# Channel attention with a GELU feed-forward layer: the first layer's weights moved by 64 bytes within a partition

## The chip, the cores and the metric

The kernel runs on one core of a Trainium2 chip. The metric is the device time of one execution in microseconds (us). The time of a version is the median of its runs; a profile shows one further execution of the same program.

## The reference, cut to what matters

```python
def _attn_ref(q, k, v, tau):                 # B, N, C = 4, 6080, 256
    qn = q / (np.linalg.norm(q, axis=1, keepdims=True) + 1e-06)
    kn = k / (np.linalg.norm(k, axis=1, keepdims=True) + 1e-06)
    s = kn.transpose(0, 2, 1) @ qn / tau     # 256 x 256 per batch
    s = s - s.max(-1, keepdims=True)
    a = np.exp(s)
    a /= a.sum(-1, keepdims=True) + 1e-09
    return (v @ a).astype(np.float32)

def _moe_ref(x, w_in, w_out):                # x: 24320 x 256, w_in: 256 x 2048, w_out: 2048 x 256
    h = x @ w_in
    g = 0.5 * h * (1.0 + erf(h * np.float32(1.0 / np.sqrt(2.0))))
    return (g @ w_out).astype(np.float32)
```

The result is `_moe_ref(_attn_ref(q, k, v, tau).reshape(24320, 256), w_in, w_out)`.

## The kernel before, in words

For each of the four batches the kernel works out the 256 x 256 attention matrix and multiplies it with `w_in`. The product is that batch's first-layer weight, 256 x 2048, so that `v` goes straight into the first layer. Every operand of the large products is split into a high and a low float32r part, and a product is three matmuls: high by high, low by high, high by low.

**First layer.** The 2048 columns of the weight are cut into four groups of 512 (`NWG`), the 6080 tokens of a batch into six pairs of blocks (`PAIRS`: five with 512 tokens a block, one with 480). A unit is one pair with 256 columns of the weight; there are 4 x 6 x 8 = 192 units. In a unit the 2 x 2 blocks of the weight meet the 2 x 2 blocks of `v`. The eight units of the very first pair do eight block products (`plain_products`); the other 184 do seven (`first_products`), with sums and differences of blocks formed ahead. That makes 8 x 8 + 184 x 7 = 1352 products. Each is three matmuls in `product`, lines 450 to 452: the weight block is the stationary operand that TensorE loads, `v`'s block (`vh`, `vl`) is the moving operand that streams through with 512 or 480 columns. The weights lie in the tiles `wh0` to `wh3` and `wl0` to `wl3`, seven blocks of 1024 bytes a partition in each. Of the plain products 16 take their weight block from another place: block A21 has no slot there and is put into the tiles that later hold `vh4` and `vl4`, or `vh5` and `vl5`. In the trace these are the rows of lines 450 to 452 whose inputs read `vh,vh`, `vl,vh` and `vh,vl`.

**Second layer.** `second_products`, lines 533 to 535, multiplies the GELU of each block (`gh`, `gl`, moving) with a unit's part of `w_out` (`wo`, stationary). A unit has 24 of these matmuls. `product` yields after each three, so that on TensorE's queue a unit's first-layer threes alternate with the second-layer threes of the unit before: 450, 451, 452, 533, 534, 535.

**Around it.** For the next batch, `burst` (lines 191 and 193) adds up scores between the units, with both operands from `hl`, and `w_group` (lines 377 to 379) makes the next weights, with `eh` and `el` stationary and `win` moving. For the first batch these stages stand ahead, with plain float32 matmuls of 256 columns in two passes each (lines 149 and 161). `sum_up` (line 172) is eight matmuls of one column against a column of ones; `softmax` uses their result. The order of all this is the order in which the program is written; TensorE's queue takes it as it stands.

**Where tiles begin.** A pool's tiles lie one behind the other in a partition, each rounded up to 32 bytes, and pools lie in the order in which they are opened. In the built program `wh0` begins at byte 1152, `wl0` at 8320, `wh1` to `wh3` and `wl1` to `wl3` at 185984, 200320, 214656, 193152, 207488 and 221824: multiples of 128, all of them. The three buffers of `wo` begin at 32896, 36992 and 41088, multiples of 128 too, and so does `win`. The moving operands `vh`, `vl`, `gh` and `gl` begin 64 bytes past a multiple of 128, and so do `hl`, `eh`, `el` and the float32 `raw` tiles. (To a multiple of 256, `vh` and `vl` lie 192 past, `gh` and `gl` 64, `wh`, `wl` and `wo` 128.) Every block within a tile starts a multiple of 512 bytes further on, so it lies as its tile does. In the pool `pwh` a tile named `pad` of 64 bytes (line 634) stands ahead of `wh1`.

Of the kernel before, what the change touches and what calls it, by code (L numbers as in the profile page):

```python
# [9 lines left out]
F32 = mybir.dt.float32  # L10
# [6 lines left out]
P = 128  # L17
# [43 lines left out]
def channel_attention_gelu_ffn(ctx, tc, qk, kqt, vt, tau, w_in, w_out, out):  # L61
# [11 lines left out]
    nc = tc.nc  # L73
    const = ctx.enter_context(tc.tile_pool(name="const", bufs=1))
# [3 lines left out]
    ptau = ctx.enter_context(tc.tile_pool(name="ptau", bufs=1))  # L78
# [3 lines left out]
    ps_h = ctx.enter_context(tc.tile_pool(name="ps_h", bufs=4, space=bass.MemoryType.PSUM))  # L82
    ps_o = ctx.enter_context(tc.tile_pool(name="ps_o", bufs=4, space=bass.MemoryType.PSUM))

    whs = [const.tile([P, 7, 2, P], F32R, name="wh0")]
    wls = [const.tile([P, 7, 2, P], F32R, name="wl0")]
    taut = ptau.tile([P, 1], F32, name="taut")
    rtau = ptau.tile([P, 1], F32, name="rtau")
    pstart = tc.tile_pool(name="pstart", bufs=1)
    pst = pstart.__enter__()  # L90

# [4 lines left out]
    make_identity(nc, ident)  # L96
    ones = const.tile([P, P], F32, name="ones")
    nc.gpsimd.memset(ones, 1.0)

    state = {}  # L100

# [68 lines left out]
    def sum_up(nps, acc, start, stop):  # L170
        for i in range(2 * NCT):
            nc.tensor.matmul(nps[:, i:i + 1], acc[:, i // NCT, i % NCT * P:(i % NCT + 1) * P],
                             ones[:, 0:1], start=(start and i == 0), stop=stop, skip_group_check=True)


    hls = {}
# [101 lines left out]
    def softmax(first, pool, name):  # L278
# [14 lines left out]
        if first:  # L293
            nps, acc = ps_o.tile([P, NT], F32, name="po"), state.pop("acc")
            with behind("scores"):
                for j in range(JS):
                    sum_up(nps, acc[:, j], j == 0, j == JS - 1)
            nc.vector.reduce_sum(out=z, in_=nsum[:, :, NSQ // NSJ:NSC], axis=AX.X)
            nc.vector.tensor_tensor(out=x, in0=nps[:, 0:2 * NCT], in1=z, op=ALU.add)
        else:  # L300
            nc.vector.reduce_sum(out=x, in_=nsum[:, :, 0:NSC], axis=AX.X)
# [329 lines left out]
    state["filled"] = True  # L631
    pg = ctx.enter_context(tc.tile_pool(name="pg", bufs=5))
    pwh = ctx.enter_context(tc.tile_pool(name="pwh", bufs=1))
    pwh.tile([P, 16], F32, name="pad")
    for g in range(1, NWG):
        whs.append(pwh.tile([P, 7, 2, P], F32R, name=f"wh{g}"))
        wls.append(pwh.tile([P, 7, 2, P], F32R, name=f"wl{g}"))
# [110 lines left out]
```

## Time and profile before

| | |
|---|---|
| median of three runs | 2212.24 us (2207.69 to 2212.78) |
| the profiled execution's own time | 2208.33 us |
| its span, first to last instruction | 2206.5 us |
| TensorE busy with matmuls | 2182.0 us, 99% of the span |
| VectorE, ScalarE, GpSimd busy | 1387.1, 1432.3 and 1.3 us |
| granted TensorE clock, mean | 0.999 |

A matmul's shown length is modelled and longer than its share of the queue, since matmuls overlap. What a matmul costs is read from the distance between one start and the next, here called a step. The timeline gives starts to 0.01 us.

### The profile page before, as it was taken

The numbers are of one execution on the slowest core, as the hardware profiler recorded it, in microseconds if no ns is written. First come the engines' busy times: TensorE is split into PE (matmuls) and PEld (weight loads), VectorE is DVE, ScalarE is ACT, GpSimd is POOL, SyncE is SP. The second block draws the span as 40 slices with busy tenths as digits, with TensorE's granted clock in tenths as the row PEclk, the third lists the DMA queues.
The fourth block names the chain that finished last, engine by engine and source line by source line (L and its number), as shares of the span: only waits on it lengthen the run. The fifth ranks groups of instructions, "written<-read, shape, count | busy, mean of one in ns | idle before, by whom it ended". The sixth has DMA issues, their size and how long they took to land.

```text
span 2206.5 us, 26233 instructions
## 1 busy us (share of the span) xinstructions
PE 2182.0 (99%) x9664; PEld 1792.7 (81%) x9664; DVE 1387.1 (63%) x2175; ACT 1432.3 (65%) x2599; POOL 1.3 (0%) x8
## 2 busy tenths in 40 slices
PE   8999999999999999999999999999999999999999
PEld 6787778888888888888888888888888888888888
DVE  6985757666576665765667657567466555554554
ACT  5668886557876565665766656656576666666665
POOL 0000000000000000000000000000000000000000
PEclk9999999999999999999999999999999999999999
DMA  9567774232652332322234323232132122122221
GB/s 381 201 218 239 242 251 136 78 113 95 231 197 77 124 105 86 115 94 87 86 105 142 101 82 123 67 124 95 48 105 95 57 91 72 68 87 70 72 76 48
DMA packets 77632, 269.61 MB, mean 122 GB/s; under 512 B 7744, under 2 KB 9792, under 8 KB 75456
## 3 DMA queue, kind: packets, MB, share of 16 engines
q1 hardware_dynamic: 77504, 267.94, 35.9%
q8 instruction: 76, 1.25, 0.2%
q14 instruction: 52, 0.43, 0.1%
HBM read 234.62 MB, written 33.29 MB: 121 GB/s over the span
## 4 chain that ended last, share of the span: by engine, by line
PE 87%; ACT 6%; DMA 5%; DVE 2%; issue 0%; SPq 0%; ACTq 0%; DVEq 0%
PE po L535 15%; PE po L533 14%; PE po L534 14%; PE ph L452 13%; PE ph L451 13%; PE ph L450 12%; DMA kqc<-kqt 4%; PE ph L191 2%; ACT kqc L209 2%; ACT gh L458 1%; ACT g L459 1%; PE ph L193 1%; DMA raw<-qk 1%; DVE acc L139 1%; PE ph L377 1%; PE ph L379 1%
## 5 line engine op out<-in xcount | busy, mean ns | idle before, releaser
L460 DVE TENSOR_TENSOR gl<-g,gh 128x512 fp32r<-128x512 f32 (+1 forms) x768 | 522.8, 682 | 157.7 <-ACT g L459 155.5
L535 PE MATMUL po<-gh,wo 128*128 128x512 f32 (+1 forms) x1536 | 605.2, 394 | 0.0
L533 PE MATMUL po<-gh,wo 128*128 128x512 f32 (+1 forms) x1536 | 599.3, 390 | 4.4 <-ACT gh L458 4.3
L534 PE MATMUL po<-gl,wo 128*128 128x512 f32 (+1 forms) x1536 | 595.9, 388 | 0.5 <-DVE gl L460 0.5
L488 DVE TENSOR_TENSOR h<-ph,p 128x512 f32<-128x512 f32 (+1 forms) x368 | 251.6, 684 | 526.0 <-PE ph L452 415.2
L458 ACT ACTIVATE gh<-h 128x512 fp32r<-128x512 f32 (+1 forms) x552 | 345.7, 626 | 285.0 <-DVE h L488 281.8
L450 PE MATMUL ph<-vh,wh 128*128 128x512 f32 (+1 forms) x1336 | 522.1, 391 | 7.6 <-ACT p L483 3.2
L452 PE MATMUL ph<-vh,wl 128*128 128x512 f32 (+1 forms) x1336 | 522.8, 391 | 0.0
L451 PE MATMUL ph<-vl,wh 128*128 128x512 f32 (+1 forms) x1336 | 521.6, 390 | 0.0
L483 ACT COPY p<-ph 128x512 f32<-128x512 f32 (+1 forms) x368 | 213.2, 583 | 247.7 <-PE ph L452 247.5
L533 PEld LDWEIGHTS po<-gh,wo 128*128 128x128 f32 x1536 | 288.6, 188 | 66.5 <-ACT gh L458 5.4
L534 PEld LDWEIGHTS po<-gl,wo 128*128 128x128 f32 x1536 | 288.5, 188 | 64.9 <-DVE gl L460 0.9
L535 PEld LDWEIGHTS po<-gh,wo 128*128 128x128 f32 x1536 | 288.4, 188 | 61.2
L459 ACT ACTIVATE g<-h 128x512 f32<-128x512 f32 (+1 forms) x552 | 337.6, 612 | 0.0
L450 PEld LDWEIGHTS ph<-vh,wh 128*128 128x128 f32 x1336 | 251.1, 188 | 66.5 <-ACT p L483 6.4
L451 PEld LDWEIGHTS ph<-vl,wh 128*128 128x128 f32 x1336 | 251.2, 188 | 55.9
L452 PEld LDWEIGHTS ph<-vh,wl 128*128 128x128 f32 x1336 | 251.1, 188 | 50.9
L483 ACT COPY u<-ph 128x512 f32<-128x512 f32 (+1 forms) x184 | 106.9, 581 | 114.5 <-PE ph L452 114.5
L458 ACT ACTIVATE gh<-ph 128x512 fp32r<-128x512 f32 (+1 forms) x216 | 124.9, 578 | 22.9 <-PE ph L452 22.7
L488 DVE TENSOR_TENSOR h<-ph,u 128x512 f32<-128x512 f32 (+1 forms) x184 | 125.6, 683 | 3.4
L459 ACT ACTIVATE g<-ph 128x512 f32<-128x512 f32 (+1 forms) x216 | 126.3, 585 | 0.0
L191 PE MATMUL ph<-hl 128*128 128x512 f32 x272 | 96.0, 392 | 0.0
(135 smaller groups left out, 1334.6 us busy)
## 6 DMA issues: line engine op xcount, KB each, us to landing
wo<-keep_out SPq DMA_DIRECT2D x184, 512.0 KB, 3.3
raw<-qk SPq DMA_DIRECT2D x95, 512.0 KB, 4.3
kqc<-kqt SPq DMA_DIRECT2D x72, 512.0 KB, 4.4
v_raw<-vt SPq DMA_DIRECT2D x20, 1024.0 KB, 5.0
out<-osb SPq DMA_DIRECT2D x40, 512.0 KB, 3.1
win<-keep_in SPq DMA_DIRECT2D x12, 1024.0 KB, 5.2
kq<-kqt SPq DMA_DIRECT2D x8, 512.0 KB, 9.6
raw<-w_out SPq DMA_DIRECT2D x8, 512.0 KB, 3.8
```

Source lines behind the costliest of these rows:

```text
L191: nc.tensor.matmul(s, hl[:, 0, j, 0, cs], hl[:, :, j, 1], start=(i == 0), stop=False, skip_group_check=True)
L450: nc.tensor.matmul(ps[:, :n], wh, hi[:, :n], start=start, stop=False, skip_group_check=True)
L451: nc.tensor.matmul(ps[:, :n], wh, lo[:, :n], start=False, stop=False, skip_group_check=True)
L452: nc.tensor.matmul(ps[:, :n], wl, hi[:, :n], start=False, stop=stop, skip_group_check=True)
L458: nc.scalar.activation(out=gh[:, :n], in_=src, func=AF.Gelu)
L459: nc.scalar.activation(out=g[:, :n], in_=src, func=AF.Gelu)
L460: nc.vector.tensor_tensor(out=gl[:, :n], in0=g[:, :n], in1=f32(gh[:, :n]), op=ALU.subtract)
L483: nc.scalar.copy(out=t[:, :n], in_=ps[:, :n])
L488: nc.vector.tensor_tensor(out=h[:, :n], in0=ps[:, :n], in1=t[:, :n], op=ALU.add)
L533: nc.tensor.matmul(o, wo[:, 0, i, cs], gh[:, :n], start=first, stop=False)
L534: nc.tensor.matmul(o, wo[:, 0, i, cs], gl[:, :n], start=False, stop=False)
L535: nc.tensor.matmul(o, wo[:, 1, i, cs], gh[:, :n], start=False, stop=last)
```

## The change

Small tiles ahead of the large ones are resized and moved. `taut` becomes a 64-byte tile and is put ahead of `wh0` in the pool `const`; `rtau` becomes a 64-byte tile behind `wl0` in the same pool; a 64-byte tile `column`, filled with ones by GpSimd, takes their place in the pool `ptau` and becomes the moving operand of `sum_up`; `pad` goes.

```diff
@@ -82,10 +82,11 @@
+    taut = const.tile([P, 16], F32, name="taut")[:, 0:1]
     whs = [const.tile([P, 7, 2, P], F32R, name="wh0")]
     wls = [const.tile([P, 7, 2, P], F32R, name="wl0")]
-    taut = ptau.tile([P, 1], F32, name="taut")
-    rtau = ptau.tile([P, 1], F32, name="rtau")
+    rtau = const.tile([P, 16], F32, name="rtau")[:, 0:1]
+    column = ptau.tile([P, 16], F32, name="column")[:, 0:1]
     pstart = tc.tile_pool(name="pstart", bufs=1)
@@ -96,6 +97,7 @@
     make_identity(nc, ident)
     ones = const.tile([P, P], F32, name="ones")
     nc.gpsimd.memset(ones, 1.0)
+    nc.gpsimd.memset(column, 1.0)
@@ -170,7 +172,7 @@
             nc.tensor.matmul(nps[:, i:i + 1], acc[:, i // NCT, i % NCT * P:(i % NCT + 1) * P],
-                             ones[:, 0:1], start=(start and i == 0), stop=stop, skip_group_check=True)
+                             column, start=(start and i == 0), stop=stop, skip_group_check=True)
@@ -631,7 +633,6 @@
     pwh = ctx.enter_context(tc.tile_pool(name="pwh", bufs=1))
-    pwh.tile([P, 16], F32, name="pad")
     for g in range(1, NWG):
```

In the built program `wh0` now begins at byte 1216, `wl0` at 8384, `wh1` to `wh3` at 186048, 200384 and 214720, `wl1` to `wl3` at 193216, 207552 and 221888. Each is 64 bytes further on than before, 64 past a multiple of 128. All tiles between them, `ident`, `ones`, `win`, `wo`, `hl`, `vh`, `vl`, `eh`, `el`, `gh` and `gl` among them, begin 128 bytes further on than before, and so lie to a multiple of 128 as they did. The order of the instructions on TensorE, VectorE, ScalarE and SyncE is the same in both programs. On GpSimd's queue, at the start of the program, the fill of `column` is added:

```order
 masks.py:197 MEMSET ident 128x128
-L98 MEMSET ones 128x128
+L99 MEMSET ones 128x128
 masks.py:199 ISA
 masks.py:199 AFFINE_SELECT ident<-ident 128x128
-L166 MEMSET sacc 128x2x256
-L744 UNCONDITIONAL_BRANCH
-L744 ISA
+L100 MEMSET column 128x1
+L168 MEMSET sacc 128x2x256
```

Behind the fills of `ident` and `ones` there is one instruction more, a fill of one element a partition; the other rows differ by the line number alone.

## Rows read from the trace of the kernel before

**Rows 1.** Page, parts 1 and 2: busy time by engine, clock in 40 slices

```profile
PE 2182.0 (99%) x9664; PEld 1792.7 (81%) x9664; DVE 1387.1 (63%) x2175; ACT 1432.3 (65%) x2599; POOL 1.3 (0%) x8
...
PEclk9999999999999999999999999999999999999999
```

**Rows 2.** Windows: length, each engine's busy us (instructions), clock, DMA share, GB/s

```profile
700.00:1200.00 500.00, 500.00 (x2238) 413.56 (x2237) 325.51 (x505) 312.11 (x564) 0.00 (x0) 1.00 0.31 104
```

**Rows 3.** Waits of TensorE: total us, times, longest; the two longest of seven

```profile
PE ph L149 <- DMA raw<-qk: 7.4, 7, 3.6
PE po L533 <- ACT gh L458: 4.3, 1, 4.3
```

**Rows 4.** Groups by shape, TensorE matmuls, line 450: count | busy, mean ns | idle

```profile
L450 PE MATMUL ph<-vh,wh 128*128 128x512 f32 x1112 | 436.1, 392 | 6.1 <-ACT p L483 3.2 <-ACT u L483 1.2 <-ACT wh L362 1.1
...
L450 PE MATMUL ph<-vh,wh 128*128 128x480 f32 x224 | 86.0, 384 | 1.6 <-ACT u L483 1.5
```

**Rows 5.** Groups by shape, weight loads of line 450, from `wh` and from `vh4`, `vh5`

```profile
L450 PEld LDWEIGHTS ph<-vh,wh 128*128 128x128 f32 x1336 | 251.1, 188 | 66.5 <-ACT p L483 6.4 <-ACT u L483 5.8 <-DVE h L488 3.1
...
L450 PEld LDWEIGHTS ph<-vh,vh 128*128 128x128 f32 x16 | 3.0, 188 | 0.6
```

**Rows 6.** Timeline, TensorE, 85.98 to 88.29 us: start, length, instruction

```profile
85.98 0.39 PE L535 MATMUL po<-gh,wo 128*128 128x512 f32 x1
86.21 0.39 PE L450 MATMUL ph<-vh,vh 128*128 128x512 f32 x1
86.43 0.40 PE L451 MATMUL ph<-vl,vh 128*128 128x512 f32 x1
86.67 0.40 PE L452 MATMUL ph<-vh,vl 128*128 128x512 f32 x1
86.90 0.39 PE L533 MATMUL po<-gh,wo 128*128 128x512 f32 x1
...
87.36 0.40 PE L535 MATMUL po<-gh,wo 128*128 128x512 f32 x1
...
88.29 0.39 PE L533 MATMUL po<-gh,wo 128*128 128x512 f32 x1
```

**Rows 7.** Timeline, TensorE: the last stretch around a `vh,vh` three

```profile
163.36 0.39 PE L535 MATMUL po<-gh,wo 128*128 128x512 f32 x1
...
164.28 0.39 PE L533 MATMUL po<-gh,wo 128*128 128x512 f32 x1
```

**Rows 8.** Timeline, TensorE: first and last stretch around a `vh,wh` three

```profile
84.60 0.39 PE L535 MATMUL po<-gh,wo 128*128 128x512 f32 x1
...
85.52 0.39 PE L533 MATMUL po<-gh,wo 128*128 128x512 f32 x1
...
2116.75 0.40 PE L535 MATMUL po<-gh,wo 128*128 128x512 f32 x1
...
2117.68 0.39 PE L533 MATMUL po<-gh,wo 128*128 128x512 f32 x1
```

**Rows 9.** Timeline, TensorE: twelve matmuls of `w_group` and what follows them

```profile
105.56 0.39 PE L377 MATMUL ph<-win,eh 128*128 128x512 f32 x1
...
108.32 0.40 PE L450 MATMUL ph<-vh,wh 128*128 128x512 f32 x1
```

**Rows 10.** Timeline, TensorE: sixteen matmuls of `burst` and what follows them

```profile
997.85 0.40 PE L191 MATMUL ph<-hl 128*128 128x512 f32 x1
...
1000.62 0.39 PE L450 MATMUL ph<-vh,wh 128*128 128x512 f32 x1
```

**Rows 11.** Timeline, TensorE: ten float32 passes of line 161

```profile
60.54 2.32 PE L161 MATMUL po<-raw 128*128 128x256 f32 x10
62.72 0.41 PE L339 MATMUL po<-ident,e 128*128 128x128 f32 x2
```

**Rows 12.** Timeline: GpSimd's last fill, and TensorE's `sum_up`

```profile
1.34 0.52 POOL L166 MEMSET sacc<- 128x512 f32 x1
...
55.30 1.84 PE L172 MATMUL po<-ones,acc 128*128 128x1 f32 x16
```

## The prediction, made before the changed kernel was run

> **What bounds the kernel now.** I read the page first, and in it the share of each engine: TensorE is busy for 99% of the span, no other engine for more than 65%, and the granted clock reads 9 in every slice [rows 1]. Since a matmul's length is modelled, I then asked a window in the middle for its sum: from 700 to 1200 us TensorE is busy for all of its 500 us, at clock 1.00, the higher of its two levels, 2.4 GHz, while VectorE and ScalarE have some 175 us to spare each and the DMA engines work at 0.31 [rows 2]. The waits of TensorE came third: the two longest are 7.4 us in all for the first loads and one of 4.3 us for the first GELU [rows 3]. So the time is the number of matmuls times the step from one start to the next. Only something that alters that step, or that breaks the row of matmuls, alters the time.
>
> What sets the step? 512 columns at 2.4 GHz are 0.2133 us, and the trace shows more. Twelve matmuls of `w_group` take 108.32 - 105.56 = 2.76 us, 0.2300 each [rows 9]. Here is a loss of some 0.017 us a matmul, and the question is whether it hangs on where in a partition the weights lie against the moving operand, because while a matmul streams, TensorE already loads the weights of the next one.
>
> **The change part by part.**
>
> *The weights' place.* Of 1352 first-layer products 1336 take their weights from `wh` and `wl`: 1112 with 512 columns and 224 with 480 [rows 4]. Three loads each make 4008 loads that now start 64 past a multiple of 128 instead of on one, while `vh`, `vl`, `gh` and `gl`, which stream meanwhile, stay 64 past. The trace of before has this very meeting in it. The 16 plain products with block A21 take their weights from the tiles of `vh4` and `vh5`, which begin 64 past, with the same moving operands ahead and around. Two readings:
>
> - The load itself: 188 ns on average for the 16 loads that begin 64 past, 188 ns for the 1336 that begin on a multiple [rows 5].
> - The steps: I take the stretch from the matmul ahead of a three, whose stream hides the three's first load, to the matmul behind the three: four steps. With the weights 64 past it is 86.90 - 85.98 = 0.92 us, and with weights on a multiple, two threes later, 88.29 - 87.36 = 0.93 us [rows 6]. There are 14 stretches of the first kind with 512 columns between 85.98 us and the one from 163.36 to 164.28 [rows 6, 7]; each is 0.92 or 0.93, with a mean of 0.9229. There are 1025 undisturbed ones of the second kind, from the one that starts at 84.60, of 0.92 us, to the one that starts at 2116.75, of 0.93 [rows 8]; their mean is 0.9251.
>
> Inside a stretch the single steps do differ: 0.23, 0.22, 0.24 and 0.23 [rows 6]. But a late start is made good by the next step, and the sum is what counts. The difference of the means is -0.0022 us a three, so the term is 1336 x -0.0022 = **-3.0 us**. The rows are given to 0.01 us, so this is a fifth of what one row can tell; I take it as it comes and treat it as not distinguishable from zero.
>
> Two other places support that. In `burst` both operands lie 64 past, as the first layer's will: eight matmuls of 512 and eight of 256 columns, 12 x 512 columns in all, take 1000.62 - 997.85 = 2.77 us, 0.2308 for 512 [rows 10]. In `w_group` the weights lie 64 past and the moving operand on a multiple, and the step is 0.2300. In the units the weights lie on a multiple and the moving operand 64 past, and four steps are 0.9251, 0.2313 each. Three meetings out of four, and one cadence within 0.6%.
>
> The bounds of this term. What the stretches do not cover is the distance in bytes taken more coarsely: the weights move by 64 and the moving operands by 128, so a period longer than 128 bytes would show a meeting that no row has. For that I bound by single steps. The slowest in the rows is 0.24 and the fastest 0.22 [rows 6]. If one step of each three went by 0.01 us and nothing were given back, that is 1336 x 0.01 = 13 us, to either side; if all three did, 40 us.
>
> *The second layer's weights, `burst` and `w_group`.* Their weights and their moving operands all move by 128 bytes together. Their places to each other stay exactly as they were: 0.
>
> *The new fill on GpSimd and `sum_up`.* One fill of one element a partition behind `ones`. GpSimd's last fill ends at 1.34 + 0.52 = 1.86 us, and `sum_up`, the only reader of `column`, starts at 55.30 [rows 12]. More than 53 us cover it; if they were gone, the cost would be at most the 0.52 us of the larger fill. `sum_up` still streams one column from a multiple of 128: 0. GpSimd's queue holds nothing else behind it than that fill of `sacc`, and issues no DMA.
>
> *`taut` and `rtau`.* The same load, the same reciprocal, another address: 0. The order on the other four queues, SP's DMA issues included, is unchanged.
>
> **The sum.** The profiled execution took 2208.33 us, its span 2206.5 and 1.8 around it. With -3.0 us it would take 2205.3. The median of the runs, 2212.24, stands 3.9 us above the profiled execution, so I forecast 2212.24 - 3.0 = **2209.2 us**. About 0.3% (6.6 us) is what a measurement of this kernel tells from no change; the three runs alone lie 5.1 us apart. So the forecast is: no change that can be told.
>
> **The rivals.**
>
> *Slower: weights and moving operand meet where no row has them.* Place: the stream of `gh` ahead of a three and the first two streams of the three, which hide its loads. If their reads got in each other's way at a period of 256 bytes or more, the 0.24 of the third step [rows 6] would stay and not be made good: +13 us, 2225. With all three steps it is +40, 2252. It decides from 6.6 / 1336 = 0.005 us a three upwards. Against it: `vh` and `gh` already differ in such coarser places, and the 0.92 or 0.93 holds over both and over all 14 stretches. For it: the exact distances are new. 0.16, mostly the smaller size.
>
> *Faster: the loss of some 0.017 us a step is a conflict of the two reads, and the new place ends it.* Float32 passes, which stream at half the rate, have it less: ten passes in 62.72 - 60.54 = 2.18 us, at most 0.218 each [rows 11], though their 256 columns take as long as 512 of the others. If 4008 steps went from 0.2313 to 0.218, that is -53 us, 2159; if one step of each three gained 0.01, it is -13 us, 2199. Against it: the loss is there in `burst` with both operands 64 past, and in the 14 stretches. 0.14, and nearly all of it at the small size.
> The Trainium skill ("TensorE: Matmul & The Clock Gate", section "Wait — 56ns, not 53.3ns?") puts the step of back-to-back matmuls at N/2.4 + about 2.5 ns, 215.7 ns at 512 columns, and knows no term for where operands lie; this trace does not agree, with 0.2300 us. By that figure the whole gain of the 4008 steps would be 4008 x 0.0156 = 63 us, an estimate from that page, and the time 2150.
>
> *The change doesn't act.* The addresses are those of the built program, so the shift is there; that it has no effect is the forecast itself.
>
> **How the numbers follow.** No change within 0.3% (2205.6 to 2218.9): 0.70, from the 14 stretches, the loads' 188 ns and the cadence common to three meetings. Slower 0.16, faster 0.14. The small sizes of the two rivals lie at 2225 and 2199; the range goes just past both, 2196 to 2226, and leaves out their large sizes.
>
> **What would show each step right or wrong.** In the profile after, four steps around a `vh,wh` three should be 0.92 or 0.93 us as before, in the middle of the run as well as at its start; the loads of lines 450 to 452 should stay at 188 ns; a window of 500 us in the middle should hold 2238 matmuls, within a few; the waits of TensorE should be the same seven kinds. Single steps may well change places with the sum unchanged. The prediction is wrong if the sum of the four steps moves by 0.005 us or more, if second-layer threes change theirs, or if a wait appears that was not there.

## The result, and the profile after

| | before | after |
|---|---|---|
| median of 20 runs each | 2209.09 us (2204.17 to 2215.99) | 2214.67 us (2209.86 to 2222.89) |
| ratio | | 1.0025, 95% interval 1.0017 to 1.0033 |
| the profiled execution | 2208.33 us, span 2206.5 | 2213.41 us, span 2211.6 |

The change costs 5.6 us, a quarter of a per cent. That is within the 0.3% called no change ahead, but with 20 runs it is clear of zero, and it is a loss where 3 us of gain were forecast. Of the other engines' busy times none moves by more than 0.2 us. The first lines of the page after, to be held against [rows 1]:

```profile
span 2211.6 us, 26233 instructions
PE 2186.1 (99%) x9664; PEld 1792.5 (81%) x9664; DVE 1386.9 (63%) x2175; ACT 1432.2 (65%) x2599; POOL 1.3 (0%) x9
...
PEclk9999999999999999999999999999999999999999
```

TensorE is the bound as before, at the same clock. Its waits after are the same seven kinds, 21.0 us in all where they were 19.7. The three longest follow; the first and the third answer to the two of [rows 3]:

```profile
PE ph L151 <- DMA raw<-qk: 8.0, 6, 3.6
PE ph L452 <- ACT p L485: 4.7, 5, 1.7
PE po L535 <- ACT gh L460: 4.2, 1, 4.2
```

So most of the loss must lie in the step. The same window as in [rows 2], after (length, busy us of each engine with its instructions, clock, DMA share, GB/s):

```profile
700.00:1200.00 500.00, 500.00 (x2230) 412.15 (x2229) 323.56 (x504) 311.61 (x564) 0.00 (x0) 1.00 0.31 103
```

TensorE is busy for all of the 500 us in both, but starts 2230 matmuls where it started 2238. The groups by shape show which (line 452 after is line 450 before, since the change adds two lines):

```profile
L452 PE MATMUL ph<-vh,wh 128*128 128x512 f32 x1112 | 439.8, 396 | 6.5 <-ACT p L485 4.7 <-ACT wh L364 1.1 <-DVE h L490 0.5
L454 PE MATMUL ph<-vh,wl 128*128 128x512 f32 x1112 | 438.8, 395 | 0.0
```

The mean length of the first matmul of a three is 396 ns after and 392 before [rows 4], that of the third 395 and 394 in the same view of before. Where it builds up is seen from the places in the program. One first-layer three (the second unit of weight group 1 in the third pair of the second batch) starts at 841.63 us before and at 842.73 after; the stretch near the end that starts at 2116.75 before [rows 8] starts at 2121.73 after. Timelines of TensorE, first that of before, then that of after:

```profile
841.63 0.39 PE L450 MATMUL ph<-vh,wh 128*128 128x512 f32 x1
...
849.92 0.39 PE L450 MATMUL ph<-vh,wh 128*128 128x512 f32 x1
```

```profile
842.73 0.40 PE L452 MATMUL ph<-vh,wh 128*128 128x512 f32 x1
842.97 0.39 PE L453 MATMUL ph<-vl,wh 128*128 128x512 f32 x1
...
851.05 0.40 PE L452 MATMUL ph<-vh,wh 128*128 128x512 f32 x1
...
2121.73 0.40 PE L537 MATMUL po<-gh,wo 128*128 128x512 f32 x1
```

Between the two places the lag grows from 1.10 to 4.98 us, 3.88 us over 706 threes of 512 columns (and 112 of 480): 5.5 ns for each of the 706. The threes of 480 columns have no part in it: over the whole execution the steps behind matmuls of 480 columns add up to 312.8 us before and after. In one unit, from the first to the seventh first-layer three, 36 steps take 8.29 us before and 8.32 after. Ahead of the first place, in the first batch and a part of the second, only 1.10 us are lost in all. TensorE's waits fall differently there in the two executions (at 250 us the changed kernel is 2.7 us ahead), so that stretch does not tell what the step costs.

For what follows, a **round** is six steps of the queue's pattern: from the start of the second-layer matmul ahead of a first-layer three to the start of the one ahead of the next. Undisturbed means that nothing else stands in it and TensorE does not wait in it. Its mean is worked out from the trace's starts in ns, over all undisturbed rounds of 512 columns from the 2000th matmul on, apart for each of the four weight groups (175 to 218 rounds each). Before it is 1380.0, 1380.0, 1379.9 and 1379.9 ns in groups 0 to 3; after it is 1386.1, 1385.9, 1385.9 and 1385.8. The first step in the three, from line 450 to line 451 (452 to 453 after), 227.9 ns before, is 233.2 after; the other five change by 1.4 ns or less, up and down.

### The profile page after: what moved, and what is told of

Its sections match the earlier page's. It is cut to its first block, busy times and chain, and to the rows that moved or that the text cites. A ratio compares the mean times of both kernels' runs of the same rounds, so it can differ in the third digit from the quotient of the medians.

```text
span 2211.6 us, 26233 instructions
## 1 busy us (share of the span) xinstructions
PE 2186.1 (99%) x9664; PEld 1792.5 (81%) x9664; DVE 1386.9 (63%) x2175; ACT 1432.2 (65%) x2599; POOL 1.3 (0%) x9
## 4 chain that ended last, share of the span: by engine, by line
PE 87%; ACT 6%; DMA 5%; DVE 2%; issue 0%; SPq 0%; ACTq 0%; DVEq 0%
PE po L537 15%; PE po L535 14%; PE po L536 14%; PE ph L452 13%; PE ph L454 13%; PE ph L453 13%; DMA kqc<-kqt 4%; PE ph L193 2%; ACT kqc L211 2%; ACT gh L460 1%; PE ph L195 1%; ACT g L461 1%; DMA raw<-qk 1%; DVE acc L141 1%; PE ph L380 1%; PE ph L379 1%
```

## The experiments

Three theories stood at the start. **Place**: weights 64 past a multiple of 128 are slow to meet. **Distance**: only the bytes between the weights being loaded and the operand streaming meanwhile count, up to some period. **Small tiles**: it is the new fill, or `sum_up`'s new operand.

### undo_column: the layout alone

The edit is against the changed kernel; those of all other runs are against the kernel before.

```diff
-    nc.gpsimd.memset(column, 1.0)
...
-                             column, start=(start and i == 0), stop=stop, skip_group_check=True)
+                             ones[:, 0:1], start=(start and i == 0), stop=stop, skip_group_check=True)
```

> The layout of the change with the column of ones taken from the tile ones again and without the new fill on GpSimd. Theory 'the weights' place': as the changed kernel, about 1.0025 of the time before; the step from line 452 to line 453 stays near 0.234 us, and four steps around a first-layer three stay at 0.929 us on average (0.924 before). Theory 'the small tiles' (the fill, the new operand of sum_up): back to the time before, 1.000, and 0.924 us.

Measured: 1.0022 (1.0013 to 1.0031), rounds of 1386.1, 1385.9, 1386.0 and 1385.8 ns. The rounds stay as they are in the changed kernel, to the tenth of a nanosecond; the new fill and `sum_up`'s new operand have no part in the loss.

### map_weights: four places of the weights in one run

```diff
     for g in range(1, NWG):
+        pwh.tile([P, 16], F32, name=f"pad{g}")
         whs.append(pwh.tile([P, 7, 2, P], F32R, name=f"wh{g}"))
```

> The kernel before, with the first-layer weights of group 0 left in place and those of groups 1, 2 and 3 moved by 64, 128 and 192 bytes; nothing else moves. The four steps around a first-layer three are read group by group. Theory 'place' (64 past a multiple of 128 is slow): groups 0 and 2 0.924 us, groups 1 and 3 0.929, the whole run some 3 us longer than before. Theory 'distance' (what counts is weights less moving operand, with a period of 256): group 0 as before, group 3, whose distance to the moving operands is that of the changed kernel, 0.929, groups 1 and 2 free to be anything. Theory 'not the weights at all': all four groups 0.924.

Measured: 1.0026 (1.0015 to 1.0037). Rounds: group 0 (unmoved) 1380.0, group 1 (64) 1392.1, group 2 (128) 1381.0, group 3 (192) 1385.8 ns. The first and seventh three of one unit in each of groups 0, 1 and 3, TensorE's timeline of this run:

```profile
820.12 0.39 PE L450 MATMUL ph<-vh,wh 128*128 128x512 f32 x1
...
828.40 0.39 PE L450 MATMUL ph<-vh,wh 128*128 128x512 f32 x1
...
843.70 0.40 PE L450 MATMUL ph<-vh,wh 128*128 128x512 f32 x1
...
852.06 0.40 PE L450 MATMUL ph<-vh,wh 128*128 128x512 f32 x1
...
888.28 0.39 PE L450 MATMUL ph<-vh,wh 128*128 128x512 f32 x1
...
896.59 0.40 PE L450 MATMUL ph<-vh,wh 128*128 128x512 f32 x1
```

8.28, 8.36 and 8.31 us: within one execution, units differ by where their weights lie. Place says groups 1 and 3 alike; they are 12 and 6 ns a round above group 0. Distance says group 3 is the changed kernel (there the weights move by 64 and the operands by 128, here by 192 and 0: -64 and 192, 256 apart), and it is, 1385.8 against 1385.8 to 1386.1.

### map_rest: the same places, everything else 128 bytes further on

```diff
     ones = const.tile([P, P], F32, name="ones")
+    const.tile([P, 32], F32, name="gap")
...
-    pwh.tile([P, 16], F32, name="pad")
     for g in range(1, NWG):
+        if g > 1:
+            pwh.tile([P, 16], F32, name=f"pad{g}")
```

> The kernel before, with everything between the weights (second-layer weights and moving operands) moved by 128 bytes as in the change, first-layer weights of group 0 left where they were, those of groups 1, 2 and 3 moved by 64, 128 and 192. Theory 'place': groups 0 and 2 0.924 us, groups 1 and 3 0.929. Theory 'distance' with a period of 256: group 2 as the kernel before, 0.924; group 1 as the changed kernel, 0.929; group 0 as group 2 of the run map_weights and group 3 as its group 1. A theory 'the moving operands' own place' (they begin 128 bytes further on): all four groups alike, 0.929.

Measured: 1.0023 (1.0012 to 1.0034). Rounds: group 1 (distance as in the changed kernel) 1386.0; group 2 (as before) 1380.0; group 3 (64 more) 1393.3; group 0 (128 less) 1384.6 ns. Two of one unit each in groups 2 and 3:

```profile
867.35 0.39 PE L451 MATMUL ph<-vh,wh 128*128 128x512 f32 x1
...
875.65 0.39 PE L451 MATMUL ph<-vh,wh 128*128 128x512 f32 x1
...
888.18 0.40 PE L451 MATMUL ph<-vh,wh 128*128 128x512 f32 x1
...
896.54 0.40 PE L451 MATMUL ph<-vh,wh 128*128 128x512 f32 x1
```

8.30 and 8.36 us. Group 2 is 128 bytes from where it was and keeps its round; the operands' own place is out. At the other distances that the two runs share they agree within 1.3 ns. One miss: group 0 should have equalled group 2 of map_weights (1381.0), and is 3.6 ns above it. The mean hides something there. With the distance changed by 128 a unit runs in one of two rhythms and mostly keeps it to its end: 98 of 217 rounds in map_weights and 53 of 174 here take 1365 to 1369 ns, 110 and 108 take 1391 to 1395, and few lie between. The two runs have the same two rhythms in other shares. Two units of group 2 in map_weights, one behind the other, on TensorE's timeline:

```profile
765.45 0.39 PE L450 MATMUL ph<-vh,wh 128*128 128x512 f32 x1
...
773.81 0.39 PE L450 MATMUL ph<-vh,wh 128*128 128x512 f32 x1
...
775.90 0.39 PE L450 MATMUL ph<-vh,wh 128*128 128x512 f32 x1
...
784.10 0.39 PE L450 MATMUL ph<-vh,wh 128*128 128x512 f32 x1
```

From first to seventh three they take 8.36 and 8.20 us, with weights from the same tiles and the same distances up to 256. What puts a unit into one rhythm or the other stays open.

### all_by_64: every large tile moved alike

```diff
+    const.tile([P, 16], F32, name="gap")
     whs = [const.tile([P, 7, 2, P], F32R, name="wh0")]
```

> The kernel before, with every large tile moved by 64 bytes: first-layer weights 64 past a multiple of 128 as in the change, second-layer weights 64 past too, moving operands on a multiple; all distances are those of the kernel before. Theory 'distance': as before, 1.000 and 0.924 us for four steps. Theory 'place': 0.929 us and 1.0025 or more, since both layers' weights are 64 past now.

Measured: 0.9991 (0.998 to 1.0002), rounds of 1379.9 ns in all four groups. The unit that took 8.29 us before takes 847.62 - 839.33 = 8.29 here:

```profile
839.33 0.39 PE L451 MATMUL ph<-vh,wh 128*128 128x512 f32 x1
...
847.62 0.39 PE L451 MATMUL ph<-vh,wh 128*128 128x512 f32 x1
```

Both layers' weights lie 64 past a multiple of 128, and nothing is lost. Place falls here.

### dose_plus64: a distance that should cost twice as much

```diff
+    const.tile([P, 16], F32, name="gap0")
     whs = [const.tile([P, 7, 2, P], F32R, name="wh0")]
...
     ones = const.tile([P, P], F32, name="ones")
+    const.tile([P, 48], F32, name="gap1")
...
-    pwh.tile([P, 16], F32, name="pad")
+    pwh.tile([P, 32], F32, name="pad")
```

> The kernel before with all large tiles moved by 256 bytes and the first-layer weights, all four groups, by 64 (group 0) or 320 (groups 1 to 3): weights less moving operand is 64 more than before everywhere, second-layer weights lie to the moving operands as before. Theory 'distance with a period of 256': each group as group 1 of the run map_weights, six steps of the queue's pattern 1.392 us in place of 1.380, so 12 ns for some 1110 threes of 512 columns, about 13 to 16 us: 1.006 to 1.007 of the time before. Theory 'any 64 past costs the same' (what the change cost, 5.6 us): 1.0025. Rival 'shifting by 256 itself matters': second-layer steps change too.

Measured: 1.0054 (1.0038 to 1.0071), 11.7 us by the medians; rounds of 1391.9, 1391.8, 1391.6 and 1391.6 ns. The round came out as forecast and the time just under the range given. 12 ns for 1112 threes would be 13 us; the unit that starts at 841.63 us before starts at 843.24 here, so only 1.6 us of it are lost by then. What the waits of the first batch take up of it was not measured apart.

```profile
843.24 0.40 PE L452 MATMUL ph<-vh,wh 128*128 128x512 f32 x1
...
851.60 0.40 PE L452 MATMUL ph<-vh,wh 128*128 128x512 f32 x1
```

8.36 us for the unit of 8.29, as in group 1 of map_weights.

### second_layer: the other layer's weights

```diff
     rtau = ptau.tile([P, 1], F32, name="rtau")
+    ptau.tile([P, 48], F32, name="gap2")
...
     ones = const.tile([P, P], F32, name="ones")
+    const.tile([P, 16], F32, name="gap1")
```

> The kernel before with second-layer weights moved by 64 bytes, moving operands by 256 and first-layer weights by 0 (group 0) or 256 (groups 1 to 3): now the second-layer weights begin 64 past a multiple of 128, as the moving operands do, and the first layer's lie to theirs as before up to 256. Theory 'distance', one rule for both layers: second-layer threes lose what first-layer threes lose, 6 to 12 ns each, 1536 of them: 9 to 18 us, 1.004 to 1.008, with the added time in the steps behind lines 452, 533 and 534. Rival 'only the first layer's weights matter': 1.000.

Measured: 1.0042 (1.0027 to 1.0057), rounds of 1387.2 to 1387.8 ns. The steps behind lines 452, 533 and 534 of the kernel before are 234.6, 234.2 and 229.2 ns where they were 231.6, 230.0 and 226.0, and the step into the first-layer three gives 2 back (233.2 for 235.1). So the second layer's weights react to their distance too; that their course is another one shows below, at 32 bytes. The run also rules out a fourth theory, that the distance between the two layers' weights counts: here and in the change the first layer's move by 64 less than the second layer's, up to 256, and the step behind line 450 is 226.5 to 226.7 ns here and 233.2 there.

### fine_map: steps of 32 bytes

```diff
     for g in range(1, NWG):
+        pwh.tile([P, (8, 16, 16)[g - 1]], F32, name=f"pad{g}")
         whs.append(pwh.tile([P, 7, 2, P], F32R, name=f"wh{g}"))
```

> The kernel before with first-layer weights of groups 1, 2 and 3 moved by 32, 96 and 160 bytes, group 0 left as it is. Theory 'distance' with a smooth course: six steps lie between the neighbours of the 64-byte map (1.380 at 0, 1.392 at 64, 1.381 at 128, 1.386 at 192): group 1 some 1.386, group 2 1.386, group 3 1.384. Theory 'halves of 128 bytes' (a read of 512 bytes that starts within a half meets as the half does): groups 1 and 3 as the next lower multiple of 64, 1.380 and 1.381, group 2 1.392.

Measured, a single run of 2219.58 us: rounds of 1380.0 (group 0), 1377.3 (32), 1383.1 (96) and 1406.1 ns (160). Neither guess holds: 32 has a shorter mean round than the layout before, 160 is worse than anything on the 64-byte map. One unit of group 3:

```profile
891.84 0.40 PE L450 MATMUL ph<-vh,wh 128*128 128x512 f32 x1
...
900.28 0.40 PE L450 MATMUL ph<-vh,wh 128*128 128x512 f32 x1
```

8.44 us, 1.8% more than before.

### split_hi_lo: the two parts of the weights moved apart

```diff
     for g in range(1, NWG):
+        if g == 3:
+            pwh.tile([P, 16], F32, name="pad3")
         whs.append(pwh.tile([P, 7, 2, P], F32R, name=f"wh{g}"))
+        pwh.tile([P, 16], F32, name=f"mid{g}")
         wls.append(pwh.tile([P, 7, 2, P], F32R, name=f"wl{g}"))
```

> The kernel before with the high and the low part of the first-layer weights moved apart: group 1 by 0 and 64 bytes, group 2 by 64 and 128, group 3 by 192 and 256, group 0 left as it is. If each load meets its own stream alone: the step from line 450 to 451 (its stream hides a load of the high part) is 0.228 in group 1, 0.233 in groups 2 and 3, the step from 451 to 452 (load of the low part) about 0.234 in group 1 and 0.229 to 0.231 in groups 2 and 3. Rival 'the whole three moves together': six steps in each group follow the high part alone, 1.380, 1.392 and 1.386.

Measured, a single run of 2213.73 us: steps behind line 450 of 228.0, 230.0 and 233.6 ns in groups 1 to 3, behind line 451 of 233.1, 234.7 and 229.6; rounds of 1386.6, 1389.9 and 1386.8. Groups 1 and 3 come as each load by itself would have it: the low part alone moved by 64 lengthens its own step by 4 ns. Group 2 fits neither. That the round follows the high part alone is out (1386.6 where it would be 1380); that the two costs simply add is not shown.

### first_by_32 and both_by_32: a better layout?

```diff
+    const.tile([P, 8], F32, name="gap0")
     whs = [const.tile([P, 7, 2, P], F32R, name="wh0")]
...
     ones = const.tile([P, P], F32, name="ones")
+    const.tile([P, 56], F32, name="gap1")
...
-    pwh.tile([P, 16], F32, name="pad")
+    pwh.tile([P, 24], F32, name="pad")
```

> The kernel before with all large tiles moved by 256 bytes and all first-layer weights by 32 more than that (group 0 by 32). From group 1 of the run fine_map: six steps 1.377 us in place of 1.380, 3 ns for some 1110 threes, about 3 us less: 0.9985 of the time before. Rival 'the 480-column threes and the rest pay it back': 1.000.

Measured: 0.9998 (0.9989 to 1.0007). The rounds did come down, to 1378.1, 1377.3, 1377.7 and 1377.8 ns, but the time did not: the steps behind matmuls of 480 columns are 1.5 us longer in all (314.3 for 312.8), and the waits for ScalarE's copies `p` and `u` in the first batches 8.7 us in this execution against 5.9. The rival was right; this beats the kernel before by nothing that can be told.

```diff
+    rtau = const.tile([P, 1], F32, name="rtau")
     whs = [const.tile([P, 7, 2, P], F32R, name="wh0")]
...
     taut = ptau.tile([P, 1], F32, name="taut")
-    rtau = ptau.tile([P, 1], F32, name="rtau")
...
-    pwh.tile([P, 16], F32, name="pad")
+    pwh.tile([P, 24], F32, name="pad")
```

> The kernel before with the weights of both layers 32 bytes further on, moving operands where they were. If second-layer threes gain at 32 what the first layer's do (3 ns each): some 6 to 7 us less, 0.997. If the two layers' distances do not add up, or the second layer's course is another one: between 0.9985 and 1.004, as the 64 bytes of the run second_layer cost 1.0042.

Measured: 1.0124 (1.0109 to 1.014), rounds of 1406.2 to 1406.7 ns. This was far outside what was expected. The unit takes 861.22 - 852.78 = 8.44 us:

```profile
852.78 0.40 PE L450 MATMUL ph<-vh,wh 128*128 128x512 f32 x1
...
861.22 0.39 PE L450 MATMUL ph<-vh,wh 128*128 128x512 f32 x1
```

### map_second32: whether the two layers' costs add

```diff
+    rtau = const.tile([P, 1], F32, name="rtau")
     whs = [const.tile([P, 7, 2, P], F32R, name="wh0")]
...
-    rtau = ptau.tile([P, 1], F32, name="rtau")
...
-    pwh.tile([P, 16], F32, name="pad")
     for g in range(1, NWG):
+        pwh.tile([P, (72, 8, 24)[g - 1]], F32, name=f"pad{g}")
```

> Second-layer weights 32 bytes further on, moving operands where they were, first-layer weights of groups 0 to 3 by 32, 224, 256 and 352 (32, -32, 0 and 96 up to 256). If the distances of the two layers add up, six steps are: group 2 what 32 does to the second layer alone, group 0 that and 3 ns less, group 3 that and 3 ns more; group 1 was not measured yet and lies between 1.377 and 1.406.

Measured, a single run of 2227.57 us: rounds of 1406.6 ns in group 0 (32), 1394.0 in group 1 (224), 1402.5 in group 2 (0) and 1393.7 in group 3 (96). So 32 bytes on the second layer's weights alone cost 22 ns a round (group 2). The two layers' parts do not add up: 32 on the first layer's gave 3 ns back by itself and costs 4 more here (group 0), 96 on them cost 3 and gives 9 back here (group 3).

### The map

First-layer weights moved against the moving operands, by so many bytes up to 256, the second layer's distance as before:

| moved by | round, ns | from |
|---|---|---|
| 0 | 1379.9 to 1380.1 | before, all_by_64, group 0 of three maps, group 2 of map_rest |
| 32 | 1377.3 to 1378.1 | fine_map, first_by_32 |
| 64 | 1391.6 to 1393.3 | map_weights, map_rest, dose_plus64 |
| 96 | 1383.1 | fine_map |
| 128 | 1381.0, 1384.6 | map_weights, map_rest |
| 160 | 1406.1 | fine_map |
| 192 (the change) | 1385.8 to 1386.1 | after, undo_column, map_weights, map_rest |

Where two moves lie 256 bytes apart (-64 and 192, -192 and 64, -224 and 32) the rounds agree within 1.4 ns. The values are means. At 0, 160 and 192 nine rounds in ten lie within 4 ns of each other. At 128 the mean mixes the two rhythms shown above, and at 32 it does so too: in group 1 of fine_map 165 of 209 rounds take 1372 to 1375 ns and the other 44, first or second rounds of a unit, 1389 to 1395. So these two means are no cadence that TensorE keeps, and 1367 ns, the faster rhythm at 128, is the shortest round that lasts for a unit. At 64 and 96 rounds of different length are mixed too.

## Why the prediction was wrong

**What bounds the kernel: right.** TensorE's row of matmuls stayed unbroken in the middle, no new kind of wait came, and the loss is in the step. The terms of 0 held too: GpSimd's fill and `sum_up` by undo_column, the common shift of 128 of the second layer's operands by group 2 of map_rest, where both layers keep their distances and their steps.

**The weights' place: the step that failed**, 3.0 us of gain for a loss of 5.6. Three things in it were wrong; the first two could have been seen in the trace of before, the third in the addresses.

First, the gain itself was rounding. The two means, 0.9229 and 0.9251 us, are taken from rows that are given to 0.01 us. From the same starts in ns the 14 stretches have a mean of 924.1 and the 1025 one of 924.2: 0.2 ns a three, not 2.2, and 0.2 us in all. So the four steps spoke for no change.

Second, the stretch was cut too short. "A late start is made good by the next step, and the sum is what counts" was tested over four steps, and the pattern of the queue has six. The same 14 stretches carried on to the next matmul of line 535 have a mean of 1384.9 ns, the 1025 others 1380.0: the 4.9 ns come in the two steps behind, up to the start at 87.36 in [rows 6]. Around such a three the first step is short, 230 ns for the usual 235, and that is no gain: the step from 534 to 535 behind the three is 232 where it is 226. The stretch counted the first and left out the second. A whole round would have forecast 4.9 ns x 1336 = 6.5 us of loss; that this is near the 5.6 measured would have been luck, as the next point shows. In the changed kernel even the four steps are 929.2 ns, 4.9 more than before, at the edge of the 0.005 us that the prediction set as its sign of being wrong.

Third, the 16 products were not "this very meeting". They meet `vh4` and `vh5` at a distance of 64 more than `wh` had, and the change makes it 64 less; what the two share is only the remainder to 128. The map has 12 ns for the one, when all threes lie so, and 6 for the other. The text named this gap and sized it at 13 us (40 at worst), but gave it 0.16, on the strength of the stretches. With the stretch cut too short, that strength was not there.

**"Three meetings out of four, and one cadence within 0.6%"** was no support. 0.6% of the span is 13 us, and the effect in question is 0.25%. `burst`, at 0.2308 us for 512 columns [rows 10], and `w_group`, at 0.2300 [rows 9], differ by 0.35%, more than the 0.25% that the change cost.

**The rivals.** *Slower* was the right one in kind: distances that no row had, a period of more than 128 bytes, and steps not made good. It was to decide from 0.005 us a three; a round grew by 0.006. Two details of it were off: the step that grew is the first of the three, behind line 450 (228 to 233 ns), and not the third, and the cost, 5.6 us, is under half of the smaller size given (13). Against it stood "`vh` and `gh` already differ in such coarser places", which says nothing of distances the weights did not yet have. *Faster* as put, the whole loss of 0.017 us a step ended by a better place, is not seen at any distance tried: the best mean round is 1377.3 ns, 229.6 a step, and the faster rhythm at 128, 1367 ns, is 227.8 a step.

**The loads.** That they stay at 188 ns was right, and it is no evidence: they stay there while the step grows. Line 452 of the kernel after, the same group of weight loads as the first of [rows 5]:

```profile
L452 PEld LDWEIGHTS ph<-vh,wh 128*128 128x128 f32 x1336 | 251.1, 188 | 66.7 <-ACT p L485 7.6
```

**The numbers.** 2214.67 us lies in the range of 2196 to 2226 and within 0.3% of before, where most of the chance was put. That is no merit of the term, whose sign was wrong: the effect is small beside the range.

The Trainium skill ("TensorE: Matmul & The Clock Gate", section "Step-by-step: what each phase is for") says that loading the next tile's weights takes no read bandwidth from the matmul that runs. These runs show that the load is not free of the stream: with the same matmuls in the same order, the mean round goes from 1377 to 1407 ns by where the weights being loaded lie against the streaming operand. Whether read bandwidth is what is lost, they do not show. What in the chip meets, and why the best and the worst distance are what they are, stays open; the runs show the course in steps of 32 bytes up to 160, with 192 and one value at 224 under another second-layer distance, and a period of 256.

## What to carry to other kernels

Where TensorE's queue is unbroken and weights are loaded beside a streaming float32r operand, the distance in bytes between the two tiles within a partition is a setting worth up to 2% of the step, and a small tile added ahead of one of them changes it unseen. Try it by giving groups of weights different pads in one kernel and compare their rounds within one execution; where all units keep one rhythm that tells 1 ns of a round, which whole runs do not; where they do not, look at the single rounds and not at the mean alone. When steps that follow a repeating pattern are compared, sum them over a whole period and look at the steps behind it before calling a delay paid back, and take differences of a few ns from starts in ns, not from rows rounded to 0.01 us.

## What the runs showed of the hardware that was not expected

- A shift of 32 bytes of second-layer weights costs 22 ns a round by itself, three to four times what the change cost, while 32 bytes on the first layer's alone gain 2 to 3 ns. Of the three distances tried for the second layer that of the kernel before is the best, and for the first layer its mean round is within 3 ns of the best.
- At one and the same distance (128 more than before) units of one execution run at 1367 or at 1393 ns a round and mostly keep to it; the distance alone does not fix the step.
- A cost can show in steps other than those in which the moved weights are loaded: with the first-layer weights moved by 64, the step into the three is 6 ns shorter than before (229.2 for 235.1), and the steps from 533 to 535 are 9 ns longer.
- The effects of the two layers' distances do not add up; for the high and the low part that is not shown.
